# A shorter first run of dummy products at the start of a fused attention and feed-forward kernel

## The chip, the cores and the metric

The kernel runs on one core of a Trainium2 chip. Its time is the device time of one launch in microseconds (us). The number that counts is the median of several runs of the same program. One further execution is recorded by the hardware profiler; all durations and dates below are from that one, and dates are counted from the start of its span.

## What is computed

There are two steps. The first is an attention with a small memory: 8 batches, 8 heads, 576 positions, 64 values a head, and 32 memory slots. The keys and values are first summed into the 32 slots with softmax weights taken from `phi`, and the queries then attend to these slots. The second step is a gated feed-forward block over the 4,608 rows that result, with 512 inputs and 1,536 inner columns.

```python
a = exp(phi - max(phi, axis=2)); a = a / (sum(a, axis=2) + 1e-09)
k_m = einsum('bhsm,bhsd->bhmd', a, k)
v_m = einsum('bhsm,bhsd->bhmd', a, v)
attn = softmax(q @ k_m.T / sqrt(64))
x = (attn @ v_m), heads side by side        # 4608 x 512
g = x @ w_gate; val = x @ w_val
out = (g * sigmoid(g) * val) @ w_out        # 4608 x 512, float32
```

## The kernel before

**Order of work.** The order is written out by hand: the program text is the order in which each engine gets its instructions[...]. Engines are TensorE (PE, with its weight loads PEld), VectorE (DVE), ScalarE (ACT), GpSimd (POOL) and SyncE (SP). PSUM has eight banks, given out by `bank` from a list of free ones, oldest first, and given back by `done`.

**Transfers.** POOL issues nearly all loads, in the order of lines 662 to 695: keys of batch 0 (L97), queries of batch 0 in two groups of heads (L107), keys of batch 1, queries of batch 1 in two groups, values of batches 0 and 1 (L101), the gate and value weights (L141: the first third in two halves each, then the second and third thirds), and then, mixed, the output weights `WO` (L156) and the inputs of batches 2 and 3 (L92, L97, L101, L114). The `phi` of batches 0 and 1 come over the queues of SP and ACT (L659, L660). SP also issues the outputs (L553) and, from batch 2 on, the transposing loads of the queries (`load_qT`, L120).

**Batches 0 and 1.** Their attention stands at the start, lines 699 to 733, before any feed-forward work exists that could fill TensorE. ACT computes the exponentials of `phi` into tiles `t_mphi` that hold each of two groups of heads in 64 of the 128 rows and zeros in the others (`phi_zeros`, `phi_exp_masked`, L190). TensorE then works through this list:

- `k_items(b)` is three items: the denominators (`p_S`, L247), the key sums (`p_kv`, L233) and the transposes of the normalized sums (`p_T`, L293), with DVE between them (L265, L269, L295).
- `q_items(b)` transposes the queries on TensorE (`p_q`, L361), and DVE copies them out (L374).
- `scores` (L384) and `z_inv` (L405) are the products of the softmax, with exponentials and logarithms on ACT (L394, L408, L410), and `norm` (L415) is its product on DVE.
- `v_direct(b)` sums the values already transposed (`p_vT`, L338), and DVE copies them to `t_kT` (L349).

**Dummy products.** Between these items stand calls of `warm(n)`. A call multiplies the constant tile `bones` by itself and puts the result in a bank that nobody reads. Its argument counts blocks of 128 columns; four blocks make one product of 512 columns, and what is left makes one shorter product. After the call the bank goes back to the head of the free list. The first call, at L699, stands ahead of all real work of TensorE and waits for nothing but `bones`. Eleven further calls, of 2 to 24 blocks, stand at lines 703 to 738.

```python
    warm(130, 0)
    k0, k1 = k_items(0), k_items(1)
    q0, q1 = q_items(0, "vvvv"), q_items(1, "vvvv")
    run(k0[:2])
    warm(8)
    run(k0[2:] + k1[:1])
```

**Feed-forward of batches 0 and 1.** From L737 on, `u_half` and `u_item` multiply the summed values with the gate and value weights (`p_u`, L435), and ACT and DVE move the results to SBUF (`t_U`, L457, L461). `gv_gate` and `flush_mul` form the gate and value products (`p_g`, `p_v`, L478), ACT's Silu (L494) and DVE's product `t_h` (L501). The output products (`p_oo`, L538) make a backlog of units that is taken up from L756 on as filling for the later batches.

**Batches 2 to 7.** The loop at L762 runs one batch at a time: scores and softmax between output products, then a stage in which gate and value products, output products and the sums of the next batch are interleaved. The output tile `t_o` has three buffers; a copy into one waits until the output transfer from it is done.

Of the kernel before, what the change touches and what calls it, by code (L numbers as in the profile page):

```python
# [14 lines left out]
def kernel(  # L15
# [57 lines left out]
    def bank(shape, dtype, name):  # L73
        tag = free.pop(0)
        t = ps.tile(shape, dtype, tag=tag, name=name)
        held[id(t)] = tag, t
        return t
# [237 lines left out]
    def k_items(b):  # L315


        def denominators():
            p = bank([128, NG], FP32, "p_S")
            kv_denominators(b, p)  # L320
            kv_reciprocal(b, p)
            done(p)

        def sums():
            p = [bank([128, D], FP32, f"p_kv{g}") for g in range(NG)]
            kv_sum(b, p, (0,))
            k_norm(b, p)
            done(*p)

        return [denominators, sums, lambda: kv_T(b, (0,))]  # L330
# [307 lines left out]
    def gv_slots(b):  # L638
        return [lambda s=s: gv_slot(b, s) for s in range(2 * NJF)]

    def warm(n, narrow=0):


        p = bank([128, DM], FP32, "p_warm")
        x = bones.rearrange("p (a c) -> p a c", a=1)
        sizes = [1] * narrow + [4] * ((n - narrow) // 4)
        sizes += [n - sum(sizes)] if n > sum(sizes) else []
        for a in sizes:
            nc.tensor.matmul(  # L649
                p[:, 0:128 * a],  # L650
                lhsT=bones,
                rhs=x.to_broadcast([128, a, 128]) if a > 1 else bones,
                start=True,
                stop=True,
            )
        free.insert(0, held.pop(id(p))[0])
# [39 lines left out]
    u_buffers(1)  # L696


    warm(130, 0)  # L699
    k0, k1 = k_items(0), k_items(1)  # L700
    q0, q1 = q_items(0, "vvvv"), q_items(1, "vvvv")
    run(k0[:2])
    warm(8)
    run(k0[2:] + k1[:1])
    warm(10)
    run(q0[:2])
    warm(3)
# [146 lines left out]
```

The softmax here doesn't subtract the row's maximum and nothing guards it: scores larger than these inputs give would overflow.

## Time and profile before

| | us |
|---|---|
| median of 6 runs | 249.04 |
| lowest and highest of them | 248.68, 249.33 |
| the profiled execution | 248.44 |
| its span, first to last instruction | 246.7 |
| TensorE busy | 239.3 |
| VectorE busy | 163.0 |
| ScalarE busy | 164.0 |
| GpSimd busy | 47.5 |
| all dummy products, busy | 14.6 |

The span begins with the first instruction and ends with the last; what lies around it, 248.44 - 246.7 = 1.74 us, belongs to the run's time as well. Busy times of TensorE are modelled, because its products are pipelined: one of 512 columns is shown with a mean of 379 ns or so, though the next may start some 0.2 us after it. So for a run of products the distance between starts is the measure, not the sum of durations. A bracket at the end of a timeline line tells how long the engine stood idle before it and what ended that.

### The profile page before, as it was taken

How to read it: one execution, taken by the hardware profiler on the slowest of the kernel's cores; microseconds unless marked ns; L12 is line 12 of the kernel's file. 1: busy time of each engine (PE TensorE's matmuls, PEld its weight loads, DVE VectorE, ACT ScalarE, POOL GpSimd, SP SyncE). 2: the span in 40 equal slices, each digit the busy share in tenths (PEclk: the TensorE clock that was granted, in tenths of full speed). 3: DMA queues.
4: the chain of work that ended last, by engine and by line, in shares of the span. 5: the costliest groups of instructions: out<-in, count | busy, mean ns of one | idle time of the engine just before them, and what ended most of it. 6: DMA issues, size and time to landing. Idle time of an engine off the chain costs nothing.

```text
span 246.7 us, 6668 instructions
## 1 busy us (share of the span) xinstructions
PE 239.3 (97%) x2621; PEld 142.9 (58%) x2621; DVE 163.0 (66%) x364; ACT 164.0 (66%) x350; POOL 47.5 (19%) x77
## 2 busy tenths in 40 slices
PE   7988999999999999999999999999999999999993
PEld 2554567775544755467645665476546655567543
DVE  4046799993437688479847788479746886587420
ACT  2637889985086567967896677866895678676201
POOL 8532522000230004053105410080005000000000
PEclk9999999999999999999999999999999999999999
DMA  6999999995999965996994699289414311310143
GB/s 213 204 206 204 201 206 208 254 251 80 195 194 246 243 67 96 215 306 114 186 251 127 96 201 257 59 154 167 89 46 119 69 43 45 85 43 4 43 128 85
DMA packets 42447, 37.00 MB, mean 150 GB/s; under 512 B 15920, under 2 KB 37168, under 8 KB 42416
## 3 DMA queue, kind: packets, MB, share of 16 engines
q0 software_dynamic: 21424, 22.42, 52.0%
q1 hardware_dynamic: 20240, 13.37, 22.9%
q10 hardware_dynamic: 752, 0.79, 0.9%
q8 instruction: 20, 0.33, 0.5%
q14 instruction: 11, 0.09, 0.1%
HBM read 42.47 MB, written 9.44 MB: 210 GB/s over the span
## 4 chain that ended last, share of the span: by engine, by line
PE 93%; DVE 3%; ACT 2%; DMA 1%; issue 1%
PE p_oo L538 38%; PE p_g L478 19%; PE p_v L478 19%; PE p_u L435 5%; PE p_warm L649 4%; PE p_kv L233 2%; DVE t_qT L374 1%; PE p_g L405 1%; PE p_g L384 1%; PE p_v L405 1%; DMA out_dram<-t_o 1%; DVE t_kT L349 1%; DVE t_A L415 1%; ACT t_E L394 1%; PE p_T L293 0%
## 5 line engine op out<-in xcount | busy, mean ns | idle before, releaser
L538 PE MATMUL p_oo<-WO,t_h 128*128 128x512 bf16 x420 | 108.7, 380 | 0.0
L494 ACT ACTIVATE t_sg<-p_g 128x288 bf16<-128x288 f32 x192 | 76.3, 413 | 34.0 <-PE p_g L478 27.1
L501 DVE TENSOR_TENSOR t_h<-t_sg,p_v 128x288 bf16<-128x288 bf16 x192 | 82.4, 452 | 17.3 <-PE p_v L478 12.9
L478 PEld LDWEIGHTS <-t_U 128*128 128x128 bf16 x768 | 73.9, 98 | 31.7 <-issue 2.7
L478 PE MATMUL p_g<-t_A,t_U 128*128 128x288 bf16 x384 | 77.6, 286 | 0.1
L478 PE MATMUL p_v<-t_A,t_U 128*128 128x288 bf16 x384 | 77.0, 286 | 0.0
L538 PEld LDWEIGHTS <-t_h 128*128 128x128 bf16 x420 | 39.5, 98 | 41.0 <-issue 5.9
L550 DVE COPY t_o<-p_oo 128x512 f32<-128x512 f32 x27 | 18.6, 691 | 31.4 <-PE p_oo L538 31.3
L459 DVE CAST t_U<-p_u 128x512 bf16<-128x512 f32 x42 | 26.7, 684 | 6.8 <-PE p_u L435 6.8
L455 ACT CAST t_U<-p_u 128x512 bf16<-128x512 f32 x30 | 15.8, 592 | 7.7 <-PE p_u L435 7.7
L548 ACT COPY t_o<-p_oo 128x512 f32<-128x512 f32 x8 | 4.7, 588 | 20.0 <-PE p_oo L538 19.9
L114 POOL DMA_DIRECT2D t_q<-in_q_dram x6 | 4.8, 801 | 60.8 <-DMA t_qT<-t_q 59.5
L649 PE MATMUL p_warm<-bones 128*128 128x512 bf16 (+2 forms) x53 | 14.6, 408 | 1.7 <-DVE bones L672 1.7
L435 PE MATMUL p_u<-W,t_kT 64*32 64x512 bf16 (+1 forms) x416 | 16.0, 365 | 0.3 <-DVE t_kT L349 0.2
L394 ACT ACTIVATE t_E<-p_g 128x288 bf16<-128x288 f32 x16 | 6.6, 412 | 8.2 <-PE p_v L384 7.7
L213 POOL COPY t_mark<-t_A 1x1 bf16<-1x1 bf16 x4 | 0.7, 179 | 58.6 <-DVE t_A L415 58.6
L415 DVE TENSOR_TENSOR t_A<-t_E,t_lz 128x576 bf16<-128x576 bf16 x16 | 11.4, 750 | 0.0
L410 ACT ACTIVATE t_lz<-t_lz 128x576 f32<-128x576 f32 x16 | 10.9, 682 | 0.5
L636 ACT ACT_TABLE_LOAD x7 | 9.0, 1283 | 1.4 <-PEq L838 1.3
L649 PEld LDWEIGHTS <-bones 128*128 128x128 bf16 x53 | 5.2, 106 | 8.0 <-issue 2.7
L461 DVE TENSOR_SCALAR t_U<-p_u,t_rS 128x512 bf16<-128x512 f32 (+1 forms) x14 | 8.8, 670 | 1.4 <-PE p_u L435 1.4
L435 PEld LDWEIGHTS <-t_kT 64*32 64x32 bf16 x416 | 4.9, 89 | 8.2 <-issue 6.7
(66 smaller groups left out, 171.2 us busy)
## 6 DMA issues: line engine op xcount, KB each, us to landing
t_kv<-in_k_dram POOLq DMA_DIRECT2D x8, 576.0 KB, 9.3
t_kv<-in_v_dram POOLq DMA_DIRECT2D x8, 576.0 KB, 13.3
out_dram<-t_o SPq DMA_DIRECT2D x23, 192.0 KB, 2.5
t_phi<-in_phi_dram POOLq DMA_DIRECT2D x6, 576.0 KB, 15.7
t_q<-in_q_dram POOLq DMA_DIRECT2D x6, 576.0 KB, 7.0
out_dram<-t_o SPq DMA_DIRECT2D x24, 128.0 KB, 2.4
WO<-in_moe_w_out_dram POOLq DMA_DIRECT2D x3, 512.0 KB, 19.3
out_dram<-t_o SPq DMA_DIRECT2D x23, 64.0 KB, 2.0
```

The source lines that it names most:

```text
L394: nc.scalar.activation(out=e[:, r], in_=p[r][:, 0:HALF], func=AF.Exp, scale=sm_scale)
L410: nc.scalar.activation(out=lz, in_=lz, func=AF.Exp, scale=-1.0)
L415: nc.vector.tensor_tensor(out=a, in0=es.pop((b, g)), in1=lzs.pop((b, g)), op=ALU.mult)
L435: nc.tensor.matmul(p[g][32 * i:32 * i + 32, o:o + n], lhsT=kTs[b][64 * g:64 * g + 64, 2, 32 * i:32 * i + 32], rhs=w_part(w, c, i, g, halve ...
L455: nc.scalar.copy(out=t, in_=p)
L459: nc.vector.tensor_copy(out=t, in_=p)
L478: nc.tensor.matmul(p[:, 0:HALF], lhsT=Us[b, c, g][:, o // 2, which, 128 * (o % 2):128 * (o % 2 + 1)], rhs=atts[b, g][:, r], start=(g == 0) ...
L494: nc.scalar.activation(out=sg, in_=gate[:, 0:HALF], func=AF.Silu)
L501: nc.vector.tensor_tensor(out=dst, in0=sg, in1=val[:, 0:HALF], op=ALU.mult)
L538: nc.tensor.matmul(mine["p"], lhsT=hts[c, jf][:, 128 * u:128 * (u + 1)], rhs=WO[jf], start=(jf == 0), stop=(jf == NJF - 1),)
L550: nc.vector.tensor_copy(out=t_o, in_=mine["p"])
L649: nc.tensor.matmul(p[:, 0:128 * a], lhsT=bones, rhs=x.to_broadcast([128, a, 128]) if a > 1 else bones, start=True, stop=True,)
```

## The change

The first call of `warm` asks for 104 blocks instead of 130. The helper also loses its second argument, which made a number of one-block products and was 0.

```diff
-    def warm(n, narrow=0):
+    def warm(n):
...
-        sizes = [1] * narrow + [4] * ((n - narrow) // 4)
+        sizes = [4] * (n // 4)
         sizes += [n - sum(sizes)] if n > sum(sizes) else []
         for a in sizes:
             nc.tensor.matmul(
...
-    warm(130, 0)
+    warm(104)
     k0, k1 = k_items(0), k_items(1)
     q0, q1 = q_items(0, "vvvv"), q_items(1, "vvvv")
     run(k0[:2])
```

The masked tiles of `phi` for batches 0 and 1 are there before and after; the difference touches only the lines shown.

## The prediction

> **What bounds the kernel now.** I read the page's share lines first, then the chain of waits, then the timeline of the first 40 us, and last the transfers with their landings.
>
> ```profile
> PE 239.3 (97%) x2621; PEld 142.9 (58%) x2621; DVE 163.0 (66%) x364; ACT 164.0 (66%) x350; POOL 47.5 (19%) x77
> ...
> PE 93%; DVE 3%; ACT 2%; DMA 1%; issue 1%
> ...
> L649 PE MATMUL p_warm<-bones 128*128 128x512 bf16 (+2 forms) x53 | 14.6, 408 | 1.7 <-DVE bones L672 1.7
> ```
>
> TensorE carries 93% of the chain that ends last, so a piece taken off its stream shortens the run, unless something with a date of its own stands further down. The third line is the dummy product: 53 of them, 14.6 us busy, and they wait for nothing but their constant. The timeline of the start, with columns start, duration, engine, line, operation:
>
> ```profile
> 1.74 9.04 PE L649 MATMUL p_warm<-bones 128*128 128x512 bf16 x33 [1.74 <-DVE bones L672]
> ...
> 5.13 0.15 PEld L649 LDWEIGHTS <-bones 128*128 128x128 bf16 x1 [0.28 <-issue]
> 5.54 4.85 PEld L649 LDWEIGHTS <-bones 128*128 128x128 bf16 x23 [0.26 <-issue]
> 5.78 4.72 ACT L190 ACTIVATE t_mphi<-t_phi 64x1152 bf16<-64x1152 f32 x4 [3.24 <-DMA t_phi<-in_phi_dram]
> ...
> 9.27 0.74 POOL L141 DMA_DIRECT2D W<-in_moe_w_gate_dram  x1 [1.63 <-DMA t_kv<-in_k_dram]
> ...
> 10.83 0.59 PE L247 MATMUL p_S<-ones,t_mphi 128*128 128x1 bf16 x18
> ...
> 11.35 0.75 PE L233 MATMUL p_kv<-t_kv,t_mphi 64*32 64x64 bf16 x72
> ```
>
> The first run of dummies (33 products) holds TensorE from 1.74 to 10.78 us, and the first real product starts 0.05 us behind it. What that product needs was there earlier: the exponentials of batch 0 are two of the four at L190, so done at 5.78 + 2 x 1.18 = 8.14, and the first keys had landed by 9.27, because the weight load that POOL issues there waited for them. So in this stretch the dummies end last, not the data. Weight loads come 0.43 us apart up to 5.54 and then 23 in 4.85 us, (4.85 - 0.15)/22 = 0.214 us apart: TensorE goes at half pace at first and then at full pace.
>
> The dated things further down are the transfers that POOL's queue streams. POOL's ninth and later issues each wait for the landing of the transfer eight places earlier, so POOL's issue times are a late reading (by some 0.3 us) of the landings:
>
> ```profile
> 24.51 0.74 POOL L141 DMA_DIRECT2D W<-in_moe_w_val_dram  x1 [2.11 <-DMA t_kv<-in_v_dram]
> ...
> 25.82 0.77 PEld L338 LDWEIGHTS <-t_kv 128*64 128x64 bf16 x36 [0.42 <-issue]
> 25.87 0.74 POOL L156 DMA_DIRECT2D WO<-in_moe_w_out_dram  x1 [0.61 <-DMA W<-in_moe_w_gate_dram]
> ...
> 26.98 0.96 DVE L349 CAST t_kT<-p_vT 64x64 bf16<-64x64 f32 x4
> 27.08 0.45 PE L435 MATMUL p_u<-W,t_kT 64*32 64x256 bf16 x9
> ...
> 27.74 0.55 PE L435 MATMUL p_u<-W,t_kT 64*32 64x256 bf16 x7 [0.21 <-DVE t_kT L349]
> ...
> 30.21 0.75 POOL L92 DMA_DIRECT2D t_phi<-in_phi_dram  x1 [0.94 <-ACT t_sg L494]
> ...
> 31.66 0.63 PE L435 MATMUL p_u<-W,t_kT 64*32 64x256 bf16 x32
> ...
> 34.96 0.74 POOL L101 DMA_DIRECT2D t_kv<-in_v_dram  x1 [1.79 <-DMA W<-in_moe_w_val_dram]
> ...
> 36.44 0.62 PE L435 MATMUL p_u<-W,t_kT 64*32 64x512 bf16 x16
> ```
>
> The reader is to see pairs: a landing, and the product that needs it 1.3 to 1.5 us later. That distance is the room TensorE has to come earlier.
>
> [...]The clock column of the page reads 9 and the clock of every stretch reads 1.00, also where the spacing is 0.43 us, so I go by the spacing.[...]
>
> **The change part by part.**
>
> 1. Instructions. 130 blocks of 128 columns are 32 products of 512 columns and one of 256; 104 blocks are 26 of 512. Seven products and their weight loads go: 6 x 512 + 256 = 3,328 columns. They are the last of the run, so at full pace: 6 x 0.214 = 1.28 us, and half of one more, 0.11 us, 1.39 us. A later run of six such products, at 24.42 to 25.89 with one lasting 0.379, gives (1.47 - 0.379)/5 = 0.218 each, so 1.42. I take 1.41. If the half pace lasts longer in some execution it does so at the front, and the same seven go from the end.
>
> 2. Dropping the unused second argument of the helper changes no instruction: it was 0 in the only call that gave it. The instruction order on POOL and SP is the same; on DVE and ACT as well, but for names. The helper puts its bank back at the head of the free list, so later tiles get the same banks. Cost 0.[...]
>
> 3. First consumers. The first products move from 10.83 to 9.42, 1.28 us after the exponentials of batch 0 (8.14). The key sums move from 11.35 to 9.94, 0.67 us after the keys' late date 9.27. The second batch's denominators move from 12.90 to 11.49, 1 us after the fourth exponential (10.50). No wait appears, so the whole 1.41 us passes on.
>
> 4. The dated transfers, "needed before", minus 1.41, against the late date: second keys 17.64 to 16.23 against 14.96; the queries of batch 1 19.50 to 18.09 against 17.70 and 21.07 to 19.66 against 18.86; values of batch 0 23.73 to 22.32 against 21.67. All fit. The values of batch 1: the weight load at 25.82 goes to 24.41 against 24.51, so a wait of 0 to 0.1 us. Behind it DVE's L349 starts at 26.98, 0.28 us after the products that it reads end (25.94 + 0.76 = 26.70), because it is still in the second L415 until 26.95; so up to 0.28 us of wait is covered. First gate weights: 27.08 goes to 25.67 against 25.87, a wait of 0 to 0.2 us. Behind it on TensorE is the same round for batch 1, which waits for DVE's t_kT anyway (0.21 us, the line at 27.74), so this wait is covered by that one. The second half of the first weights: 31.66 to 30.25 against 30.21. The next gate and value weights: 36.44 to 35.03 against 34.96. Both just fit. The transfers' own dates, issue plus time to landing, are some 0.3 us earlier still (values of batch 1: 6.86 + 17.4 = 24.26). The third weight pair, freed by 40.19, is used at 45.60. Sum of uncovered waits: 0 to 0.15 us; I take 0.02.
>
> 5. The second stage. The queries of batch 2 land at 40.19 + 20.1 = 60.29, SP then transposes from 60.38 and that lands 5.0 us later, 65.4. The scores that use it start at 69.22 and go to 67.81: room 2.4 us. Keys and values of batch 3 land at 81.3 (67.54 + 13.7) and are summed from 85.53, so 84.12. POOL's query load at 66.02 keeps its date, since it waits for that transpose. Outputs: t_o has three buffers, SP issues the first output only after the transpose, 63.55, with 2.0 to 2.5 us to landing, so by 66.1; the fourth copy moves from 68.23 to 66.82. It fits by about 0.7 us, and ACT's next work after it is 0.77 us later anyway. From there on every issue follows TensorE, and the shift reaches the end.
>
> Sum: -1.41 + 0.02 = -1.39 us. Against the profiled execution: 248.44 - 1.39 = 247.05 (span 246.7 to 245.3; 1.74 us lie around the span and stay). That execution is 0.60 us under the median of the six runs, 249.04, so the median becomes 247.65, 0.56% less.
>
> **The rivals.**
>
> A, the full shift as above: 247.65, with 0.25 us either way for the two products' pace and for how far two medians differ (the six runs before span 0.65).
>
> B, part of it is given back to landings. For: in step 4, four pairs fit by 0.2 us or less, and one execution's landings are one sample. If the stream is 0.5 us late, the values of batch 1 cost 0.1 + 0.5 - 0.28 = 0.3 us and the pairs at 30.2 and 35.0 about 0.45 us, not added, since a wait at one moves the next: saving 0.9, time 248.15. Against: the issue dates that I compare with are already the late reading.
>
> C, a transfer hides all of it: the landing would have to be 1.4 us later than shown at some pair, or a pair that I left out rules. Time 249.0. Nothing in the chain of waits speaks for it: its DMA share, 1%, is the output at the end.
>
> D, slower. One mechanism: TensorE falls back to half pace between 9.4 and 26 us, where it runs small products with gaps (busy 1.68 of 2.00 us in the stretch 18 to 20), because 1.4 us of dense work ahead of that stretch is gone.[...] Against: all gaps there are 0.4 us or less, the stretch itself is unchanged, and the remaining first run still holds TensorE for 7.6 us.
>
> E, that the run isn't the limit at all, because the first keys end last. 9.27 is before the new end, 9.37, so the edit does what its words say; if the keys came 0.5 us later the loss would be that, which is in B.
>
> **How the numbers follow.** A 0.66, B 0.23, C and E together 0.06, D 0.05. The prediction is A's 247.65. The range runs from A's lower end, 247.3, to 248.5, most of B, leaving out C and D. A change within 0.2% (0.5 us) can't be told from none here. Faster by more than that takes A and nearly all of B: 0.87. Same 0.08: C and the rest of B. Slower 0.05: D.
>
> **What would show it.** Right: the first run has 26 products and ends at 9.37; p_S starts at about 9.42 and the key sums at about 9.94 with no wait for keys; the rounds at 31.66 and 36.44 are found at about 30.25 and 35.03; POOL's issues up to 40.19 keep their dates within 0.3 us; the transpose still starts near 60.4 and the end is 1.4 us earlier. Wrong: idle time ahead of L338, or L435 put down to t_kv or W (B); the product at 36.44 unmoved (C); weight loads 0.43 us apart after 9.4 us (D).

## The result and the profile after

| | before | after |
|---|---|---|
| median, us | 248.96 (35 runs) | 247.31 (16 runs) |
| lowest and highest, us | 247.93, 249.61 | 246.85, 248.75 |
| ratio, 95% interval | | 0.9943, 0.9931 to 0.9954 |
| profiled execution, us | 248.44 | 247.81 |
| its span, us | 246.7 | 246.0 |

The ratio says 0.57% less, which is 1.42 us of 248.96; its interval is 1.15 to 1.72 us less. The two medians alone are 1.65 us apart: the ratio on record is not the quotient of the two medians, and how it is formed isn't recorded, so both are given below where they differ. The two profiled executions are only 0.63 us apart, and their spans only 0.7. That gap between the runs and the profile is the first thing to explain. The page of the changed kernel, at the places shown for the one before:

```profile
PE 238.6 (97%) x2614; PEld 142.4 (58%) x2614; DVE 163.0 (66%) x364; ACT 164.2 (67%) x350; POOL 47.5 (19%) x77
...
PE 93%; DVE 3%; ACT 2%; DMA 1%; issue 1%
...
L649 PE MATMUL p_warm<-bones 128*128 128x512 bf16 (+2 forms) x46 | 14.0, 435 | 1.7 <-DVE bones L672 1.7
```

Seven dummy products are gone (46 for 53), and TensorE carries the chain as before. But their mean rose from 408 to 435 ns. The timeline of the start tells why:

```profile
1.73 8.43 PE L649 MATMUL p_warm<-bones 128*128 128x512 bf16 x26 [1.73 <-DVE bones L672]
...
6.83 0.15 PEld L649 LDWEIGHTS <-bones 128*128 128x128 bf16 x1 [0.27 <-issue]
7.19 2.47 PEld L649 LDWEIGHTS <-bones 128*128 128x128 bf16 x12 [0.21 <-issue]
9.43 0.74 POOL L141 DMA_DIRECT2D W<-in_moe_w_gate_dram  x1 [1.79 <-DMA t_kv<-in_k_dram]
...
10.22 0.59 PE L247 MATMUL p_S<-ones,t_mphi 128*128 128x1 bf16 x18
...
10.73 0.75 PE L233 MATMUL p_kv<-t_kv,t_mphi 64*32 64x64 bf16 x72
...
24.63 0.74 POOL L141 DMA_DIRECT2D W<-in_moe_w_val_dram  x1 [2.11 <-DMA t_kv<-in_v_dram]
...
25.32 0.76 PE L338 MATMUL p_vT<-t_mphi,t_kv 128*64 128x64 bf16 x36
...
27.12 0.55 PE L435 MATMUL p_u<-W,t_kT 64*32 64x256 bf16 x7 [0.21 <-DVE t_kT L349]
```

In this execution the weight loads stay 0.43 us apart up to 6.83 and only then close up; before, they did so at 5.54. So the first real product starts at 10.22, only 0.61 earlier than the 10.83 of before, and not 1.41. From there the two profiles run alike: L233 0.62 earlier (10.73 for 11.35), the second round of L435 0.62 (27.12 for 27.74), the end 0.7. POOL's issues up to 40 us have kept their dates within 0.2 us.

### The profile page after: what moved, and what is told of

The parts are those of the page before. It is cut to its first block, busy times and chain, and to the rows that moved or that the text cites. A ratio compares the mean times of both kernels' runs of the same rounds, so it can differ in the third digit from the quotient of the medians.

```text
span 246.0 us, 6654 instructions
## 1 busy us (share of the span) xinstructions
PE 238.6 (97%) x2614; PEld 142.4 (58%) x2614; DVE 163.0 (66%) x364; ACT 164.2 (67%) x350; POOL 47.5 (19%) x77
## 4 chain that ended last, share of the span: by engine, by line
PE 93%; DVE 3%; ACT 2%; DMA 1%; issue 1%
PE p_oo L538 38%; PE p_g L478 20%; PE p_v L478 19%; PE p_u L435 5%; PE p_warm L649 4%; PE p_kv L233 2%; DVE t_qT L374 1%; PE p_g L405 1%; PE p_g L384 1%; PE p_v L405 1%; DMA out_dram<-t_o 1%; DVE t_kT L349 1%; DVE t_A L415 1%; ACT t_E L394 1%; PE p_T L293 1%
## 5 line engine op out<-in xcount | busy, mean ns | idle before, releaser
L435 PE MATMUL p_u<-W,t_kT 64*32 64x512 bf16 (+1 forms) x416 | 16.0, 365 | 0.3 <-DVE t_kT L349 0.2
L649 PE MATMUL p_warm<-bones 128*128 128x512 bf16 (+2 forms) x46 | 14.0, 435 | 1.7 <-DVE bones L672 1.7
L415 DVE TENSOR_TENSOR t_A<-t_E,t_lz 128x576 bf16<-128x576 bf16 x16 | 11.4, 751 | 0.0
L435 PEld LDWEIGHTS <-t_kT 64*32 64x32 bf16 x416 | 4.9, 89 | 8.2 <-issue 6.7
```

The lines of the kernel that those rows point to most:

```text
L415: nc.vector.tensor_tensor(out=a, in0=es.pop((b, g)), in1=lzs.pop((b, g)), op=ALU.mult)
L435: nc.tensor.matmul(p[g][32 * i:32 * i + 32, o:o + n], lhsT=kTs[b][64 * g:64 * g + 64, 2, 32 * i:32 * i + 32], rhs=w_part(w, c, i, g, halve ...
L649: nc.tensor.matmul(p[:, 0:128 * a], lhsT=bones, rhs=x.to_broadcast([128, a, 128]) if a > 1 else bones, start=True, stop=True,)
```

## The experiments

Theory 1: the dummies of the first run lie on the path up to the date at which the data are there, and further cuts bring little. Theory 2 came with the profile after: TensorE's change to full pace comes at another date in each execution, and the span is the start of the first real product plus a constant. Theory 3 came with a second profile and concerns the output buffers. Each diff starts from the version named beside it.

**Less still in the first run: 78 blocks**, from after.

```diff
-    warm(104)
+    warm(78)
```

> First run of dummies cut once more by 26 blocks, to 78. Theory 1 (dummies lie on the path only until the data are there): of the further 1.41 us only 0.2 to 0.6 us comes through in executions in which TensorE changes to full pace early, because the key sums would then wait for keys at 9.3 us and the value products of batch 1 at 24.5 us; more in executions that change late. Median 246.7 to 247.1. Rival (nothing waits, each block counts): 245.9. Rival D (less dense work ahead, TensorE falls back to half pace): 248 or more, with weight loads 0.43 us apart after 9 us.

Measured 246.92 us beside 248.66 for the kernel before: ratio 0.9941, interval 0.9923 to 0.9959. A second 26 blocks off bring little beside the first (0.9943), and neither rival fits: it isn't 1.4 us more, and the median isn't slower. The products of TensorE in its timeline, with what they waited for:

```profile
9.16 0.74 PE L233 MATMUL p_kv<-t_kv,t_mphi 64*32 64x64 bf16 x72 [0.41 <-DMA t_kv<-in_k_dram]
...
15.99 0.75 PE L233 MATMUL p_kv<-t_kv,t_mphi 64*32 64x64 bf16 x72 [0.59 <-DMA t_kv<-in_k_dram]
...
24.65 0.76 PE L338 MATMUL p_vT<-t_mphi,t_kv 128*64 128x64 bf16 x36 [0.49 <-DMA t_kv<-in_v_dram]
...
26.14 0.62 PE L435 MATMUL p_u<-W,t_kT 64*32 64x256 bf16 x16 [0.41 <-DMA W<-in_moe_w_gate_dram]
...
34.91 0.62 PE L435 MATMUL p_u<-W,t_kT 64*32 64x512 bf16 x16
```

Here the transfers are the limit, one after the other: both keys, the values of batch 1, the first weights. The round at 34.91 was at 36.44 before, 1.53 us earlier; the second profile of 78 blocks, below, has it at 34.95, though its first product came 1.35 us later than in this one. So about 1.5 us is all that the start gives while the loads arrive as they do.

**The same columns taken elsewhere**, from before: the first run keeps 130 blocks, and the call of 24 ahead of the values of batch 1 goes.

```diff
-    warm(24)
```

> The kernel before with its first run of 130 blocks kept, and the later call of 24 blocks ahead of the value products of batch 1 taken out instead: nearly the same number of dummy columns, elsewhere. Theory 1: those dummies stand beside VectorE's chain (two L415, then L349) and beside the landing of the values at 24.3 us, so the round at 27.74 us still waits for t_kT and nothing moves: 248.7 to 249.1. Rival (a dummy column costs the same wherever it stands): 1.3 us less, 247.7.

Measured 249.29 us beside 248.66: ratio 1.0019, interval 1.0006 to 1.0033. There is no gain, so the rival is out. The timeline of TensorE shows where the columns went:

```profile
24.84 1.33 PE L338 MATMUL p_vT<-t_mphi,t_kv 128*64 128x64 bf16 x72
26.55 0.41 PE L435 MATMUL p_u<-W,t_kT 64*32 64x256 bf16 x8
28.37 0.28 PE L435 MATMUL p_u<-W,t_kT 64*32 64x256 bf16 x1 [1.42 <-DVE t_kT L349]
28.86 0.55 PE L435 MATMUL p_u<-W,t_kT 64*32 64x256 bf16 x7 [0.21 <-DVE t_kT L349]
```

The 1.3 us of dummies have become a wait of 1.42 us for VectorE's t_kT. From the first real product (11.94) to the last round shown (28.86) it is 16.92 us, and 16.91 in the kernel before (10.83 to 27.74). Why the runs came out 0.06 to 0.33% slower isn't seen in the profile, whose span is its first product plus 235.9 us, as before. The mean granted clock of a run, the share of TensorE's full pace that was recorded over it, points to a part of it: it is 0.992 or 0.993 in eight of the 22 runs, which took 249.32 to 249.99 us, and never under 0.996 in the 31 runs of the kernel before. So those eight seem to have lost TensorE's full pace for a while; where they lost it isn't recorded. The median of the other 14 is 248.95.

**The other way, 156 blocks**, from after.

```diff
-    warm(104)
+    warm(156)
```

> First run lengthened to 156 blocks, 26 more than before and 52 more than after: 6.5 products more than before at full pace. Theory 1 and its rival of no waits alike: 1.41 us over before, 250.4, since data wait for TensorE all the more. If landings gave back part of the shift after the change, this step is larger than the measured one from 130 to 104.

Measured 250.08 us beside 248.66, 1.42 more: ratio 1.0066, interval 1.0048 to 1.0084. Its change of pace (5.51) comes as in the profile of before (5.54), and p_S starts at 12.20 for 10.83, 1.37 us later. By the ratio it is 1.64 us more (1.19 to 2.09). The step from 130 to 104 was 1.65 us by the medians and 1.42 by the ratio. The two steps can't be told apart, so nothing shows that landings gave back a part of the shift.

**No first run to speak of, 8 blocks**, from after.

```diff
-    warm(104)
+    warm(8)
```

> Only two products are left in the first run, so TensorE stands idle from about 2.7 us to the exponentials at about 8.1 us and does the first real work at half pace. Theory 1: the start is bound by the data as with 78 blocks, but weight loads and products go at half pace[...] from 8.1 us, which costs 1 to 3 us: 248 to 250. Rival (first dummies only fill time): same as with 78 blocks, about 247.

Measured 249.31 us: ratio 1.0037, interval 1.0017 to 1.0057. TensorE starts p_S at 7.24 us but is slow:

```profile
11.91 1.23 PE L649 MATMUL p_warm<-bones 128*128 128x512 bf16 x3
...
25.33 0.97 PE L338 MATMUL p_vT<-t_mphi,t_kv 128*64 128x64 bf16 x36
...
27.76 0.76 PE L338 MATMUL p_vT<-t_mphi,t_kv 128*64 128x64 bf16 x36
```

The three dummies took 0.70 us in the kernel before (at 13.36), and both of the values' sums 0.76. Its first round of L435 comes at 28.90, 2.8 us after that of 78 blocks; the profiled execution, 250.45 us, is one of its two slowest. The dummies do work: what they buy is the pace.

**The changed kernel again, 78 blocks again, 52 blocks, and the kernel before again**, for more profiles.

> The changed kernel itself once more, for a second profile. Theory 2 (the date at which TensorE changes to full pace differs between executions, 4.7 to 7.7 us in the profiles so far, and each 0.43 us of it costs 0.21 us; all else follows the first real product): the span is the start of p_S plus 235.8 us, to 0.2 us. If the change of pace comes by 5.5 us, p_S starts at 9.4 and the span is 245.2; if at 7.2, 10.2 and 246.0. Ratio to before 0.993 to 0.995. Rival (the profile's 0.7 us is the true gain and the medians are chance): 248.0, span 246.0 whatever the date.

> 78 blocks again, beside the changed kernel on the same chip. Theory 1 with 2 (data limit at about 1.5 us below before, and the run of 78 ends ahead of the data in nearly every execution): 0 to 0.4 us below the 104 blocks, with a narrower spread of its runs, lowest runs alike. Rival (more blocks off, more gain): 1.4 us below.

> 52 blocks. Theory 2: at half pace 13 products take 5.5 us and end at 7.3 us, so the change of pace still falls into the dummies or close behind, and the data limit holds: 0 to 0.8 us above 78 blocks, 247.0 to 247.8. Rival (half pace reaches the real work as with 8 blocks): 248.5 to 249.3.

> The kernel before once more, one look for a second profile. Theory 2: span is the start of p_S plus 235.8 us, to 0.2 us, wherever the change of pace falls; weight loads 0.43 us apart up to some date between 4.7 and 7.7 us. Rival: the change of pace comes at the same date, 5.5 us, as in the first profile.

The changed kernel gave 247.57 beside 248.98, ratio 0.9944, interval 0.9927 to 0.9960: the gain repeats. 78 blocks gave 247.04, ratio 0.9926 (0.9905 to 0.9946), 0.5 us under the 104 beside it, though the intervals overlap. Its six runs spread wider than those of 104, 246.49 to 247.99 for 247.29 to 248.20, where a narrower spread and equal lowest runs had been expected. The kernel before, in a single run, had 248.80 and a span of 247.0 with p_S at 11.03: the constant is 235.97, as theory 2 has it.

52 blocks is a miss: 248.90, ratio 1.000 (0.9980 to 1.0019), its runs from 247.23 to 250.61. The stretches of its start, with the columns stretch, length, busy time of PE, PEld, DVE, ACT and POOL, granted clock, DMA share and GB/s:

```profile
6.00:8.00 2.00, 1.68 (x13) 0.64 (x11) 0.00 (x0) 1.98 (x2) 1.64 (x3) 1.00 1.21 207
8.00:10.00 2.00, 1.23 (x82) 1.11 (x83) 0.20 (x2) 1.95 (x3) 0.61 (x1) 1.00 1.28 201
10.00:12.00 2.00, 1.85 (x24) 0.98 (x23) 1.04 (x4) 0.67 (x1) 0.88 (x2) 0.61 1.29 204
12.00:14.00 2.00, 1.94 (x15) 1.21 (x14) 0.75 (x2) 0.00 (x0) 0.74 (x1) 0.50 1.21 209
...
18.00:20.00 2.00, 1.94 (x51) 1.33 (x38) 0.90 (x3) 1.73 (x5) 1.00 (x2) 0.50 1.22 209
20.00:22.00 2.00, 1.94 (x29) 1.26 (x26) 1.79 (x4) 0.72 (x3) 0.22 (x1) 0.83 1.22 212
```

This is rival D of the prediction, at half the blocks of the change: the dummies end before the data come, TensorE is busy 1.68 and 1.23 of 2.00 us while it waits, and the granted clock falls to 0.50. By the clock record of the trace it rises at 7.04 us, falls at 10.45 and is back at 20.69. I had expected the waiting to be harmless.

The runs without a profile show the same. The mean granted clock of the 20 runs is 0.964 to 0.996; the three at 0.965 or less took 250.08 to 250.61 us, the three at 0.992 or more 247.23 to 247.35. No run of the kernel before beside them is under 0.997. (In the profiles with means of 0.996 to 0.999 the only fall lies behind the last product: in the first one of 78 blocks, 0.997, at 243.58 us.) Of 78 blocks one run in each six has lost pace as well, with 0.986 and 0.993, and it is the slowest of its six (247.71 and 247.99); of the changed kernel none in 31, the lowest mean being 0.997. So the loss came more often with fewer dummies: in none of 31 runs with 104 blocks, in 2 of 12 with 78 and in 19 of 20 with 52 (mean clocks of 0.993 or less). What decides it in a single run isn't shown: in the two profiles of 52 and of 78 blocks (the first one) the dummies end nearly together, at 7.32 and 7.54 us, and only that of 52 falls.

The second profile of the changed kernel broke theory 2: p_S starts at 9.16, the earliest of the 104s, and the round of L435 that was at 36.44 is at 34.77, the full 1.67 us earlier; but the span is 246.4 and not 245.0. VectorE's timeline shows the loss:

```profile
70.33 0.69 DVE L550 COPY t_o<-p_oo 128x512 f32<-128x512 f32 x1 [1.25 <-PE p_oo L538]
...
75.91 0.69 DVE L550 COPY t_o<-p_oo 128x512 f32<-128x512 f32 x1 [4.88 <-DMA out_dram<-t_o]
...
76.52 1.42 DVE L415 TENSOR_TENSOR t_A<-t_E,t_lz 128x576 bf16<-128x576 bf16 x2
...
77.85 1.88 DVE L459 CAST t_U<-p_u 128x512 bf16<-128x512 f32 x3
```

An output copy waits 4.88 us for a free t_o buffer, with the softmax product L415 and the copies of p_u queued behind it, and TensorE waits for VectorE at 76.65 (0.30 us) and 78.59 (0.79 us). The outputs issued at 66.1 to 68.0 us took 8.8 to 9.6 us to land here. In the first profile of the changed kernel those of 66.2 to 68.6 took 5.2 to 6.7, and there the copy didn't wait.

**Five output buffers**, with 104, 78 and 130 blocks.

```diff
-                    t_o = work.tile([128, DM], FP32, tag="to", name="t_o")
+                    t_o = work.tile([128, DM], FP32, tag="to", bufs=5, name="t_o")
...
-                    t_o = work.tile([128, h], FP32, tag="to", name="t_o")
+                    t_o = work.tile([128, h], FP32, tag="to", bufs=5, name="t_o")
```

> The changed kernel with five buffers for the output tile in place of three. In the second profile of the changed kernel VectorE stood 4.9 us before an output copy until an output transfer was done, and TensorE lost 1.4 us between 61 and 85 us. Theory 3 (coming earlier brings the output transfers together with the loads that are issued at 65.6 us, and in some executions this wait gives back up to 1.4 us): no such wait, median 0.2 to 0.6 us under the changed kernel beside it, and its slower runs gone. Rival (one odd execution, the wait does not matter for the median): equal within 0.2 us.

> 78 blocks and five output buffers: the version that should be fastest. Theory 3 with theory 1: 246.5 to 246.9, by 0.2 to 0.4 us under 78 blocks with three buffers. Rival: same as with three, 246.9 to 247.1.

> The kernel before with five output buffers. Theory 3: with TensorE later by 1.4 us the wait is rare, so within 0.2 us of the kernel before. Rival (the wait is as frequent there): 0.2 to 0.6 us less.

> The changed kernel beside its version with five buffers on the same chip, for the direct comparison and a third profile. Ratio to before 0.993 to 0.996. Theory 3: where its profile shows no wait of an output copy for a transfer, the span is the start of p_S plus 235.8 us, plus what TensorE waited for loads before 28 us.

| blocks, buffers | median, us | ratio to before | interval |
|---|---|---|---|
| before beside them: 130, 3 | 248.96 | | |
| 130, 5 | 248.62 | 0.9992 | 0.9977 to 1.0007 |
| 104, 3 (the change) | 247.68 | 0.9953 | 0.9935 to 0.9970 |
| 104, 5 | 247.53 | 0.9951 | 0.9935 to 0.9966 |
| 78, 5 | 246.80 | 0.9919 | 0.9897 to 0.9940 |

Theory 3 falls as far as the median goes: with 104 blocks five buffers give 247.53 for 247.68, which isn't a difference here, and its highest run (250.15) isn't lower. The wait for a buffer stands in one of the five profiles with three buffers and 104 or 78 blocks; how often it comes in the runs without a profile isn't recorded. The run of 250.15 us is the profiled one, and its trace shows another late transfer:

```profile
113.45 0.80 PE L233 MATMUL p_kv<-t_kv,t_ephi 64*32 64x128 bf16 x72 [1.46 <-DMA t_kv<-in_v_dram]
```

The sums of a later batch wait 1.46 us for its values. In the third profile of the changed kernel they start at 111.45 without a wait. The output copies of the two profiles are 0.48 us apart before this place and 2.00 behind it, and about as far apart at the end. Step 5 of the prediction had checked the loads of batch 3, summed from 85.53 us, but none as late as this.

78 blocks with five buffers is the fastest version tried, 2.2 us under the kernel before on the same chip. With three buffers 78 blocks gave 0.9941 and 0.9926, so how much of that the buffers do isn't shown.

## Why the prediction was right

247.65 us was forecast and 247.31 measured; the forecast gain was 1.39 us, and by the ratio it is 1.42. That these two agree to 0.03 us is in part luck: the interval is 1.15 to 1.72 us, the medians are 1.65, 1.41 and 1.28 us apart in the three comparisons of the two kernels, and the 247.31 lies at the very edge of the range that began at 247.3. The cause is that of the prediction. By its own steps:

Step 1, seven products at full pace, 1.41 us: right. Pairs of profiles with the change of pace at nearly the same date give it directly. Where the weight loads close up at 7.69 (130 blocks, without the later 24) p_S starts at 11.94; where they do so at 7.69 too (104 blocks, five buffers) at 10.54: 1.40. With the third profile of 104 blocks, 7.67 and 10.48, it is 1.46, and the pair 156 and 130 gives 1.37.

Its sum against the profiled execution, 247.05 with a span of 245.3, was off: 247.81 and 246.0. The step took the half pace at the front as the same length in both executions. The weight loads closed up at 5.54 in one and at 7.19 in the other; after 2 us the changed kernel's profile has twelve weight loads 0.43 us apart (2.14 to 6.83) and that of before eight (2.14 to 5.13). Each of the four more costs 0.43 - 0.214 = 0.22 us, together 0.86, which is the part of the 1.41 that is missing at p_S (0.61 came through) within 0.06. The text said that a longer half pace sits at the front and leaves the seven products at full pace. That holds, but it shifts a single profile by more than half the gain.

The profiles with 104 blocks and more, by the start of p_S, show how far the rest is a constant (all in us):

| kernel, blocks | weight loads close up at | p_S starts | span | difference |
|---|---|---|---|---|
| before, 130 | 5.5 | 10.83 | 246.7 | 235.9 |
| before again, 130 | 6.0 | 11.03 | 247.0 | 236.0 |
| after, 104 | 7.2 | 10.22 | 246.0 | 235.8 |
| after, third, 104 | 7.7 | 10.48 | 246.4 | 235.9 |
| 156 | 5.5 | 12.20 | 248.3 | 236.1 |
| 130, five buffers | 6.4 | 11.28 | 247.1 | 235.8 |
| 130, without the later 24 | 7.7 | 11.94 | 247.8 | 235.9 |
| after, second, 104 | 5.1 | 9.16 | 246.4 | 237.2 |

The last line is the one with the wait for an output buffer. The profile of 104 blocks with five buffers, 10.54 and 248.4, falls out of the row too, with 237.9; it is that kernel's highest run, 250.15, with the wait of 1.46 us for values shown above.

Steps 2 and 3: right; no wait at the first consumers, and the shift at p_S is the shift at L233.

Step 4, dated transfers, 0 to 0.15 us: right in size. The second profile of the changed kernel tests it, since TensorE was early in it: it waited 0.20 us for the second keys and 0.35 us for the first gate weights, and nothing was lost of that by 34.77. It wasn't foreseen that the second keys would be among the late ones: 1.27 us of room was counted there. How narrow the rest was shows with 78 blocks, where five waits of 0.16 to 0.59 us take the place of the 26 blocks. Rival B is so not the outcome of this change but that of the next cut, and C is out.

Step 5: the start of the transpose (60.06, forecast 60.38) and its room were right. The price of the outputs was too low: 2.0 to 2.5 us to landing was taken from the page, a median over the whole run. Those issued up to 65.7 us take 2.0 to 3.8 us, but from 66 us on, beside the loads that POOL issues from 65.6, they take 5.2 to 9.6 in the first two profiles of the changed kernel, and up to 6.8 in that of the kernel before. The copy that waits is the sixth, not the fourth that was checked. The medians with three and with five buffers don't show this cost.

Rival D was an estimate of the author's: no profile of the kernel before shows a fall to half pace ahead of its last product. It didn't come with 104 blocks: by their mean clock none of 31 runs lost its pace (0.997 or more). It came in one run of each six with 78 (0.986 and 0.993), and with 52 the times of the 20 runs follow it (0.964 to 0.996). The prediction's reason against it, that all gaps are 0.4 us or less, isn't tested by this: with 52 blocks the pace fell with gaps of up to 0.62 us.

## What to carry to other kernels

In this kernel 26 blocks of dummies cost their full time, 1.37 to 1.46 us, where they ended later than the data of the next real product came: compare the end of the run with the landing of what that product reads, and cut back to there. Cut further, and here the transfers took over first (78 blocks, five waits of 0.16 to 0.59 us), and then the pace was lost in 19 of 20 runs (52). Before two single profiles are compared, look at when each of them goes to full pace; here that date alone moved a span by about 0.8 of the 1.41 us.

## What was not expected of the hardware

- The first product starts at 1.73 or 1.74 us in every profile, but the change to full pace came, by the clock record of the traces, between 4.65 us (78 blocks) and 7.77 us (104 with five buffers), and with 8 blocks only at 25.89. With 52 blocks or more it lay 2.9 to 6.0 us after the first product. What sets the date isn't shown. The changes that the records give lie at 7.04, 10.45, 20.69 and 245.97 us with 52 blocks, so 3.41, 10.24 and 225.28 us apart, and at 4.65 and 243.58 with 78, 238.93 us apart.
- The fall to half pace with 52 blocks came without a long idle time: in the 3.41 us from 7.04 to 10.45 TensorE was busy for 2.30 us, and the longest idle time ahead of a product was 0.62 us. With 78 blocks it was busy for 2.54 us in as long a stretch, from 8.06 to 11.47, and kept its pace.
- The granted clock reads 1.00 in stretches in which products are spaced at half pace (8 blocks, 10 to 24 us), and 0.50 only after a fall from full pace (52 blocks, 12 to 20 us): the record begins with the first change, at 5.51 us in the kernel before, whose weight loads are 0.43 us apart ahead of it.
- The second keys landed later where TensorE was early: POOL's issue that waits for them came at 16.23 and 16.38 (78 blocks, two profiles), 16.36 (104, the second) and 16.45 (52), but at 14.96 and 15.13 in the first profiles of before and after. With 8 blocks, at half pace, it came at 15.30. The cause is open.
